# Softmax of a decode-attention step: eight accumulating exps replaced by one shift on VectorE, two whole-tile exps on ScalarE and a sum on VectorE

## The chip, the cores and the metric

The kernel runs on one core of one Trainium2 chip. The metric is the device time of one execution in microseconds (us), as a median of runs. A ratio is the mean time of one kernel's fast runs over that of the other's of the same rounds, so it is not quite the ratio of the medians that are quoted beside it.

Engine names in the profile: PE is the matrix engine, PEld its weight loads, DVE is VectorE, ACT is ScalarE, SPq is the queue that issues the loads. "L691" is a line of the kernel. PSUM is the memory that PE writes its results to here, SBUF the on-chip memory that the loads fill. The span is the length of the profiled execution. The granted clock is the share of its full clock that PE was given; "full clock" below means 1.00.

## The reference, cut to what matters

One token goes through a modulated layer norm, attention over a long cache, and a gated FFN. Attention is the large part: 32 query heads share 4 K/V heads of 65,536 rows.

```python
q = (h @ wq)                                   # 32 heads of 128, one row
scores = einsum('bhqd,bhkd->bhqk', q, k) * 128 ** -0.5     # k: 4 heads x 65536 x 128, each shared by 8 heads
p = softmax(scores, axis=-1)
o = einsum('bhqk,bhkd->bhqd', p, v)
x = x + ga * (o @ wo)
h = layernorm(x) * (1 + cb) + sb
out = x + gb * ((gelu(h @ w_gate) * (h @ w_up)) @ w_down)
```

Every byte of K, V and the weights is used once.

## The kernel before

The cache is worked off in 32 steps. A step takes 64 K tiles and 64 V tiles of 128x128 (2 MB of K and 2 MB of V) for 8 heads. PE transposes the K tiles in four groups T(0..3), DVE (three groups) and ACT (one) move them from PSUM to SBUF, and PE then computes the scores QK into one PSUM bank and, after the exps, P times V. Stages of three steps are interleaved:

```python
# PE, step i: T and MT/MB belong to i and i-1, QK to step i-1, PV to step i-2
T(0); QK(0); T(1); QK(1); PV(0); T(2); QK(2); QK(3); PV(1); T(3); PV(2); MT(); PV(3); MB()
# PV(0) waits for the V load and for ex, the exps of its step
```

```python
# DVE and ACT, step i (cut)
E(0)                                   # DVE: evict 16 transposed K tiles
OC()                                   # DVE: copy out an attention output
E(1); E(2)                             # DVE
# with j = i - 1; the scores lie in sc_ps[:, (j % 2) * 512 : +512] as (tile n, head h)
m1[s].done(dve.tensor_reduce(m_col[:, j % 2, :].unsqueeze(2), scv, AX.X, ALU.max))
...                                    # max over partitions through PE (MT, MB)
v_mc[j] = DVE.done(dve.tensor_copy(mneg[:, j, :], b6[:, 256:256 + REP]))   # -scale * max, on all partitions
E(3)                                   # ACT: evict the last 16 tiles
AC.wait(v_mc[j], pt.get(("PV", j - SITES)))
for h in range(REP):                   # REP = 8 heads
    ins = act.activation(
        p_sb[:, s, :, h], scv[:, h, :], ACT.Exp,
        bias=mneg[:, j, h:h + 1], scale=scale, accum_out=z_all[:, j, h:h + 1],
    )
ex[s].done(ins)
```

The loads go through one queue in a fixed order into ten 2 MB slots. A load is issued as soon as PE has released its slot:

```python
def issue_ready():
    while issued[0] < len(loads):
        j = loads[issued[0]]
        if any(q.freed is None for q in j.prev):
            return
        SP.wait(*(q.freed for q in j.prev))
        sp.dma_start(j.view, j.src).then_inc(j.tok[0], 16)
        issued[0] += 1
```

## Time and profile before

| | before |
|---|---|
| median | 440.44 us (440.28 to 440.68) |
| profiled span | 438.8 us |
| read from HBM | 185.60 MB |
| PE / DVE / ACT busy | 351.7 / 176.2 / 146.4 us |

These lines of the profile page give the busy time of each engine, the bytes, and by fortieths of the span (in tenths) the granted PE clock and the busy share of the DMA engines.

```profile
PE 351.7 (80%) x7107; PEld 318.4 (73%) x7107; DVE 176.2 (40%) x300; ACT 146.4 (33%) x553; POOL 11.7 (3%) x25
...
PEclk9955555959777986869955899556995597659855
DMA  8999999999999999999999999999999999999995
...
HBM read 185.60 MB, written 0.00 MB: 423 GB/s over the span
```

PE has the highest busy share of the compute engines, but the row of the DMA is the one that is full from the first slice to the last but one. The windows view has the exact numbers: window, then busy time of PE, PEld, DVE, ACT and POOL with instruction counts, then the granted clock, the DMA share and GB/s.

```profile
200.00:225.00 25.00, 20.55 (x478) 20.02 (x478) 12.42 (x20) 11.89 (x51) 0.00 (x0) 0.87 1.01 432
225.00:250.00 25.00, 25.00 (x485) 24.72 (x484) 11.48 (x17) 9.21 (x35) 0.00 (x0) 0.59 1.01 436
...
388.00:392.00 4.00, 1.33 (x28) 1.20 (x29) 3.15 (x6) 0.00 (x0) 0.00 (x0) 0.50 1.01 429
```

In the first window PE idles for 4.5 us; in the second, at a granted clock of 0.59, it is busy throughout; in the third PE has almost nothing to do, because the softmax is being closed. The DMA moves about 430 GB/s in all three. The Trainium skill, "DMA: Bandwidth & Descriptors", section Specifications, names 435 GB/s as the ceiling of the fabric; the trace's 429 to 436 GB/s lie at it (other windows of 15 and 25 us read up to 442, so page and trace agree to about 2%).

What the change removes is this pair of groups (line, engine, operation, output and input, count; then busy time and mean ns of one; then the idle time before them):

```profile
L691 ACT ACTIVATE p_sb<-sc_ps,mneg 128x64 bf16<-128x64 f32 x256 | 83.5, 560 | 3.9 <-DVE mneg L686 3.9
L691 ACT ACTIVATION_READ_ACCUMULATOR p_sb<-sc_ps,mneg 128x1 f32 x256 | 77.1, 365 | 0.0
```

The two groups overlap in time, so they are not to be added: the timeline shows one exp starting every 0.29 us. Here are the ends of one step's exps and what stands behind them (timeline: start, duration, instruction):

```profile
209.14 0.54 ACT L691 ACTIVATE p_sb<-sc_ps,mneg 128x64 bf16<-128x64 f32 x1
...
211.36 0.39 ACT L691 ACTIVATION_READ_ACCUMULATOR p_sb<-sc_ps,mneg 128x1 f32 x1
...
211.85 0.54 PE L625 MATMUL b<-p_sb,slots 128*128 128x8 bf16 x16 [0.58 <-issue]
```

PE sat idle for 0.58 us before its first PV matmul, until just after the eighth exp's accumulator was read (211.36 + 0.39 = 211.75 us). So the exps are taken to be on PE's path in this step (the profile names no releaser, `<-issue`; the times fit).

PE's waits, longest in total first (engine, line, what it waited for: us in total, times, longest):

```profile
PE b L625 <- DMA slots<-in_A_v_cache_dram: 11.2, 12, 2.0
...
PE kt_ps L561 <- DMA slots<-in_A_k_cache_dram: 10.3, 5, 5.1
...
PE b L625 <- issue: 6.4, 8, 2.4
...
PE b L625 <- ACT p_sb L691: 3.0, 1, 3.0
```

PE waits 21.5 us for K and V loads in the loop and at most 9.4 us for the exps.

### The profile page before, as it was taken

The numbers are of one execution on the slowest core, as the hardware profiler recorded it, in microseconds if no ns is written. First come the engines' busy times: TensorE is split into PE (matmuls) and PEld (weight loads), VectorE is DVE, ScalarE is ACT, GpSimd is POOL, SyncE is SP. The second block draws the span as 40 slices with busy tenths as digits, with TensorE's granted clock in tenths as the row PEclk, the third lists the DMA queues.
The fourth block names the chain that finished last, engine by engine and source line by source line (L and its number), as shares of the span: only waits on it lengthen the run. The fifth ranks groups of instructions, "written<-read, shape, count | busy, mean of one in ns | idle before, by whom it ended". The sixth has DMA issues, their size and how long they took to land.

```text
span 438.8 us, 15336 instructions
## 1 busy us (share of the span) xinstructions
PE 351.7 (80%) x7107; PEld 318.4 (73%) x7107; DVE 176.2 (40%) x300; ACT 146.4 (33%) x553; POOL 11.7 (3%) x25
## 2 busy tenths in 40 slices
PE   0547449998989889898799989999989999557554
PEld 0214139998989879798799989899988999434234
DVE  4102013545444644455444466345563365142100
ACT  1000001343435634344613553444654434600000
POOL 8100000000000000000000000000000000000000
PEclk9955555959777986869955899556995597659855
DMA  8999999999999999999999999999999999999995
GB/s 332 427 435 428 430 429 432 432 433 425 430 445 420 453 414 455 408 445 438 410 448 415 445 419 442 427 435 432 430 437 424 439 423 433 432 427 431 424 425 237
DMA packets 11957, 185.89 MB, mean 424 GB/s; under 512 B 1568, under 2 KB 1568, under 8 KB 1952
## 3 DMA queue, kind: packets, MB, share of 16 engines
q1 hardware_dynamic: 11632, 185.61, 98.8%
q8 instruction: 13, 0.21, 0.2%
q10 hardware_dynamic: 304, 0.01, 0.0%
q14 instruction: 8, 0.07, 0.0%
HBM read 185.60 MB, written 0.00 MB: 423 GB/s over the span
## 4 chain that ended last, share of the span: by engine, by line
DMA 60%; PE 35%; DVE 2%; issue 1%; SPq 1%; ACT 1%; POOL 0%
DMA slots<-in_A_v_cache_dram 39%; PE kt_ps L561 18%; DMA slots<-in_A_k_cache_dram 10%; DMA slots<-in_B_w_down_dram 7%; PE b L625 7%; PE sc_ps L581 6%; DMA slots<-in_w_mod_dram 4%; PE kt_ps L392 2%; PE b L605 1%; SPq L234 1%; PE b L372 1%; ACT p_sb L691 1%; PE b L595 1%; DVE kt_sb L751 0%; PE sc_ps L453 0%
## 5 line engine op out<-in xcount | busy, mean ns | idle before, releaser
L561 PE MATMUL kt_ps<-ident,slots 128*128 128x128 bf16 x2048 | 179.5, 258 | 11.0 <-DMA slots<-in_A_k_cache_dram 10.3
L561 PEld LDWEIGHTS kt_ps<-ident,slots 128*128 128x128 bf16 x2048 | 154.9, 118 | 12.7 <-issue 9.8
L660 DVE COPY kt_sb<-kt_ps 128x2048 bf16<-128x2048 bf16 x96 | 117.6, 1225 | 108.6 <-PE kt_ps L561 108.5
L660 ACT ACTIVATE kt_sb<-kt_ps 128x2048 bf16<-128x2048 bf16 x32 | 60.1, 1877 | 183.3 <-PE kt_ps L561 183.3
L625 PE MATMUL b<-p_sb,slots 128*128 128x8 bf16 x2176 | 75.8, 168 | 20.6 <-DMA slots<-in_A_v_cache_dram 11.2
L625 PEld LDWEIGHTS b<-p_sb,slots 128*128 128x128 bf16 x2176 | 69.8, 100 | 23.3 <-DMA slots<-in_A_v_cache_dram 12.3
L691 ACT ACTIVATE p_sb<-sc_ps,mneg 128x64 bf16<-128x64 f32 x256 | 83.5, 560 | 3.9 <-DVE mneg L686 3.9
L691 ACT ACTIVATION_READ_ACCUMULATOR p_sb<-sc_ps,mneg 128x1 f32 x256 | 77.1, 365 | 0.0
L581 PE MATMUL sc_ps<-q_buf,kt_sb 128*128 128x8 bf16 x2112 | 69.9, 167 | 0.5 <-issue 0.5
L581 PEld LDWEIGHTS sc_ps<-q_buf,kt_sb 128*128 128x128 bf16 x2112 | 67.9, 100 | 0.6 <-issue 0.6
L392 PE MATMUL kt_ps<-slots,h_pad 128*32 128x512 bf16 x176 | 17.1, 510 | 14.3 <-DMA slots<-in_A_wq_dram 6.3
L684 DVE TENSOR_REDUCE mg<-b 8x1 f32<-8x128 f32 x32 | 8.9, 279 | 37.1 <-PE b L595 37.1
L679 DVE TENSOR_REDUCE m_col<-sc_ps 128x8 f32<-128x512 f32 x32 | 21.8, 681 | 4.7 <-PE sc_ps L581 4.7
L392 PEld LDWEIGHTS kt_ps<-slots,h_pad 128*32 128x32 bf16 x176 | 5.0, 112 | 24.1 <-DMA slots<-in_A_wq_dram 8.3
L392 PE MATMUL kt_ps<-slots,s_pad 128*32 128x512 bf16 x96 | 12.5, 553 | 9.3 <-DMA slots<-in_w_mod_dram 9.3
L392 PEld LDWEIGHTS kt_ps<-slots,s_pad 128*32 128x32 bf16 x96 | 3.6, 119 | 17.3 <-DMA slots<-in_w_mod_dram 12.6
L605 PE MATMUL b<-negi,mg 8*128 8x8 f32 x66 | 15.8, 309 | 0.0
L605 PEld LDWEIGHTS b<-negi,mg 8*128 8x128 f32 x66 | 12.7, 239 | 2.2
L453 PEld LDWEIGHTS sc_ps<-identf,kt_sb 128*128 128x128 f32 (+1 forms) x48 | 7.6, 204 | 8.2 <-DVE kt_sb L774 4.3
L453 PE MATMUL sc_ps<-identf,kt_sb 128*128 128x128 f32 (+1 forms) x48 | 9.1, 352 | 4.5 <-DVE kt_sb L774 2.4
L686 DVE COPY mneg<-b 128x8 f32<-128x8 f32 x32 | 5.3, 167 | 18.1 <-PE b L605 18.1
L372 PE MATMUL b<-u_col,slots 128*128 128x1 bf16 x224 | 6.6, 165 | 6.5 <-DMA slots<-in_B_w_down_dram 5.9
(97 smaller groups left out, 84.9 us busy)
## 6 DMA issues: line engine op xcount, KB each, us to landing
slots<-in_A_k_cache_dram SPq DMA_DIRECT2D x16, 4096.0 KB, 20.3
slots<-in_A_v_cache_dram SPq DMA_DIRECT2D x32, 2048.0 KB, 26.5
slots<-in_w_mod_dram SPq DMA_DIRECT2D x8, 1536.0 KB, 17.5
slots<-in_A_wq_dram SPq DMA_DIRECT2D x4, 2048.0 KB, 35.2
slots<-in_A_wo_dram SPq DMA_DIRECT2D x4, 2048.0 KB, 32.5
slots<-in_B_w_gate_dram SPq DMA_DIRECT2D x4, 1792.0 KB, 21.9
slots<-in_B_w_up_dram SPq DMA_DIRECT2D x4, 1792.0 KB, 23.6
slots<-in_B_w_down_dram SPq DMA_DIRECT2D x3, 2048.0 KB, 29.1
```

What stands on the lines that cost most here:

```text
L372: ins = pe.matmul(bank[:, j:j + 1], view[:, kk, j * P:(j + 1) * P], rhs[:, k0 + kk:k0 + kk + 1], start=first, stop=True, skip_group_check= ...
L392: ins = pe.matmul(out, pad[:, k, :], jb.view[:, kk, c0:c0 + ROW], start=k <= last_k[0], stop=k >= last_k[1], skip_group_check=True,)
L453: ins = pe.transpose(dst[:, i * w:i * w + n], src[:, a], identf[0:src.shape[0], 0:n])
L561: ins = pe.transpose(kt_ps[:, half * 2048 + t * P:half * 2048 + (t + 1) * P], j_k[i - i % KU].view[:, i % KU * CH + b * TB + t, :], ident[ ...
L581: ins = pe.matmul(sc_ps[:, base + n * REP:base + (n + 1) * REP], kt_sb[:, j % 2, n, :], q_buf[:, j % SITES, :], start=True, stop=True,)
L605: ins = pe.matmul(b6[:, 256:256 + REP], mg8[:, j % 2:j % 2 + 1].to_broadcast([REP, P]), negi[:, :], start=True, stop=True,)
L625: ins = pe.matmul(b7[:, s * REP:(s + 1) * REP], j_v[j].view[:, n, :], p_sb[:, s, n, :], start=(n == 0), stop=(n == CH - 1),)
L660: ev[i % SITES][b].done(act.activation(dst, src, ACT.Copy) if E_ is AC else dve.tensor_copy(dst, src))
L679: m1[s].done(dve.tensor_reduce(m_col[:, j % 2, :].unsqueeze(2), scv, AX.X, ALU.max))
L684: m2[s].done(dve.tensor_reduce(mg8[:, j % 2:j % 2 + 1], b6[0:REP, 32:32 + P], AX.X, ALU.max))
L686: v_mc[j] = DVE.done(dve.tensor_copy(mneg[:, j, :], b6[:, 256:256 + REP]))
L691: ins = act.activation(p_sb[:, s, :, h], scv[:, h, :], ACT.Exp, bias=mneg[:, j, h:h + 1], scale=scale, accum_out=z_all[:, j, h:h + 1],)
```

## The change

Its intent is to relieve ACT. All 8 heads get their own maximum subtracted by DVE in one pass over the score tile in PSUM, in place. ACT then needs no bias and no accumulator, so one instruction covers all 8 heads: one exp writes P as bf16 and a second writes the exp as f32 back into PSUM, and DVE sums that one. Sixteen ACT records a step become two; DVE gets two passes over 128x512 f32.

```diff
+            def Z():
+                j = i - 2
+                if not 0 <= j < NC:
+                    return
+                zv = sc_ps[:, (j % 2) * 512:(j % 2) * 512 + CH * REP].rearrange("p (n h) -> p h n", h=REP)
+                DVE.wait(v_ze[j])
+                v_z[j] = DVE.done(dve.tensor_reduce(z_all[:, j, :].unsqueeze(2), zv, AX.X, ALU.add))
+
             E(0)
             OC()
             E(1)
+            Z()
             E(2)
...
                 v_mc[j] = DVE.done(dve.tensor_copy(mneg[:, j, :], b6[:, 256:256 + REP]))
+                DVE.wait(v_mc[j])
+                v_sh = DVE.done(dve.scalar_tensor_tensor(
+                    scn.rearrange("p (n h) -> p n h", h=REP), scn.rearrange("p (n h) -> p n h", h=REP), scale,
+                    mneg[:, j, :].unsqueeze(1).to_broadcast([P, CH, REP]), ALU.mult, ALU.add))
             E(3)
             if 0 <= j < NC:
-                AC.wait(v_mc[j], pt.get(("PV", j - SITES)))
-                for h in range(REP):
-                    ins = act.activation(
-                        p_sb[:, s, :, h], scv[:, h, :], ACT.Exp,
-                        bias=mneg[:, j, h:h + 1], scale=scale, accum_out=z_all[:, j, h:h + 1],
-                    )
-                ex[s].done(ins)
+                AC.wait(v_sh, pt.get(("PV", j - SITES)))
+                ex[s].done(act.activation(p_sb[:, s, :, :].rearrange("p n h -> p (n h)"), scn, ACT.Exp))
+                v_ze[j] = AC.done(act.activation(scn, scn, ACT.Exp))
```

(Cut: the definition of `scn`, the score tile of step j, two empty dictionaries, and the wait for the last sum before the final rescaling.)

More of the change, by code (lines that the diff above doesn't have):

```diff
@@ L648, in emit_all @@
         v_mc = {}
+        v_ze = {}
+        v_z = {}
         def others_step(i):
@@ L685, in others_step @@
                 DVE.wait(pt[("MB", j)])
+                scn = sc_ps[:, (j % 2) * 512:(j % 2) * 512 + CH * REP]
                 v_mc[j] = DVE.done(dve.tensor_copy(mneg[:, j, :], b6[:, 256:256 + REP]))
+                DVE.wait(v_mc[j])
+                v_sh = DVE.done(dve.scalar_tensor_tensor(
+                    scn.rearrange("p (n h) -> p n h", h=REP), scn.rearrange("p (n h) -> p n h", h=REP), scale,
+                    mneg[:, j, :].unsqueeze(1).to_broadcast([P, CH, REP]), ALU.mult, ALU.add))
             E(3)
             if 0 <= j < NC:
-                AC.wait(v_mc[j], pt.get(("PV", j - SITES)))
-                for h in range(REP):
-                    ins = act.activation(
-                        p_sb[:, s, :, h], scv[:, h, :], ACT.Exp,
-                        bias=mneg[:, j, h:h + 1], scale=scale, accum_out=z_all[:, j, h:h + 1],
-                    )
-                ex[s].done(ins)
+                AC.wait(v_sh, pt.get(("PV", j - SITES)))
+                ex[s].done(act.activation(p_sb[:, s, :, :].rearrange("p n h -> p (n h)"), scn, ACT.Exp))
+                v_ze[j] = AC.done(act.activation(scn, scn, ACT.Exp))
         PE.wait(t1, v_negi, v_q, v_zero)
@@ L732, in emit_all @@
         v_w = AC.done(act.activation(w_all[:, :, :], w_all[:, :, :], ACT.Exp))
-        DVE.wait(v_w, *(ex[i % SITES].tok(seen_by(i)) for i in range(NC - SITES, NC)))
+        DVE.wait(v_w, v_z[NC - 1])
         v = DVE.done(dve.tensor_tensor(z_all[:, :, :], z_all[:, :, :], w_all[:, :, :], ALU.mult))
```

## The prediction

> **What bounds the kernel now.** The DMA. The page counts 185.6 MB read; from 5 us to 432 us the windows view gives a DMA share of 0.98 to 1.04 in every stretch, through attention loop, softmax tail (384 to 404 us) and FFN. 185.6 MB at the loop's about 431 GB/s is 430.6 us; the slow first 5 us and the 5.3 us after the last weights land (433.5 us) make up the rest of the 438.8 us span. The Trainium skill, "DMA: Bandwidth & Descriptors", Specifications, gives a fabric ceiling of 435 GB/s; the trace sits at it. PE (80% busy) is a close second: a loop step (about 9.7 us of DMA for 4.19 MB) takes PE 8.0 to 8.6 us at full clock, 11.1 us at the granted 0.5; the queue's slack of about 10 us (K loads take 20.3 us to landing, 9.7 us of it their own) evens this out. DVE (40%) and ACT (33%) have room.
>
> **What the change does per step (32 steps).**
> - Removed on ACT: 8 exps of 128x64 with accumulator reads, 2.63 us together (chain of waits).
> - Added on ACT: two 128x512 exps. A 128x512 f32 ACT copy out of PSUM takes 0.597 us, so about 1.1 to 1.2 us together. ACT busy falls from 146 to about 102 us.
> - Added on DVE: the shift in PSUM, 0.69 us (as the 128x512 f32 PSUM copy), and the sum, 0.68 us (as the max over the same tile with the same stride). DVE busy rises from 176 to about 220 us (50%).
> - P is ready about 1.4 us after the max instead of 2.6.
>
> **How much is on the critical path.** Little. At full clock PE waits 0.6 us a step for the exps before the first PV (timeline, 211.2 to 211.8 us); at clock 0.5 not at all. So PE's full-clock steps shrink by 0.6 us, but PE then only waits longer for the next K or V load, since the DMA is full. In the tail the last exps shorten by about 1.2 us (381.2 to 383.9 us); the FFN is gated by weights landing until 433.5 us, so this too is swallowed.
>
> **New costs that could show.** At full clock the shift ends about 209.5 us, where the next step's first eviction on DVE starts at 209.6. The sum stands between second and third eviction: 1.23 + 0.68 = 1.9 us against the 1.75 us that PE needs there, so the third eviction and the max slip 0.15 us, against 0.45 us of slack. At half clock there are 3 us of room. I expect no DMA starvation.
>
> **Prediction: 440.2 us, 8 in 10 between 439.0 and 441.8.** Faster by over 2%: 0.01; within 2%: 0.97; slower: 0.02.
>
> **What would show it.** DMA share still 0.98 to 1.04 in every loop window and the last weights landing at 433 to 434 us; ACT busy about 100, DVE about 220 us; shift and sum near 0.69 us; PE's wait for the exps gone and its waits for K and V loads grown by as much; last-ending chain still mainly DMA.
>
> **What would make it wrong.** (1) Longer DMA waits leave PE idle longer and its granted clock (mean 0.733) falls; if it runs at 0.5 for several pairs of steps, slots are freed late and DMA windows drop below 0.97: slower. (2) Shift or sum cost about twice as much (strided view, PSUM read and write in one pass), pushing evictions and PE. [...]

## The result, and the profile after

| | before | after |
|---|---|---|
| median of 6 runs | 440.44 us | 440.53 us (440.32 to 440.67) |
| ratio of fast runs | | 1.0001 (95%: 0.9989 to 1.0014) |
| PE / DVE / ACT busy | 351.7 / 176.2 / 146.4 us | 347.2 / 216.3 / 100.4 us |

Nothing changed in the time. Executions over 1.5% slower than the fastest of the same kernel are left out of the means. The page's rows after, the same as shown before:

```profile
PE 347.2 (79%) x7107; PEld 310.8 (71%) x7107; DVE 216.3 (49%) x364; ACT 100.4 (23%) x105; POOL 11.7 (3%) x25
...
PEclk9955558886677886968579599887859989568655
DMA  8999999999999999999999999999999999999995
...
HBM read 185.60 MB, written 0.00 MB: 423 GB/s over the span
```

46 us of ACT work went, 40 us of DVE work came, and the DMA row is the same to the digit. The windows shown before have, after:

```profile
200.00:225.00 25.00, 23.74 (x436) 23.32 (x437) 14.48 (x24) 7.94 (x9) 0.00 (x0) 0.60 1.01 433
225.00:250.00 25.00, 22.89 (x547) 22.42 (x546) 16.12 (x25) 7.67 (x7) 0.00 (x0) 0.84 1.02 437
...
388.00:392.00 4.00, 3.94 (x40) 1.64 (x44) 0.00 (x1) 0.00 (x0) 0.00 (x0) 0.50 0.99 420
```

The new groups cost what same-sized passes had cost before:

```profile
L706 ACT ACTIVATE p_sb<-sc_ps 128x512 bf16<-128x512 f32 x32 | 19.1, 597 | 19.0 <-DVE sc_ps L700 19.0
L700 DVE SCALAR_TENSOR_TENSOR sc_ps<-sc_ps,mneg 128x512 f32<-128x512 f32 x32 | 22.4, 700 | 1.1
L678 DVE TENSOR_REDUCE z_all<-sc_ps 128x8 f32<-128x512 f32 x32 | 21.8, 681 | 2.2 <-ACT sc_ps L707 2.2
...
L707 ACT ACTIVATE sc_ps<-sc_ps 128x512 f32<-128x512 f32 x32 | 18.9, 592 | 0.0
```

PE's waits after:

```profile
PE kt_ps L561 <- DMA slots<-in_A_k_cache_dram: 15.4, 6, 5.1
PE b L625 <- DMA slots<-in_A_v_cache_dram: 13.9, 13, 2.1
...
PE b L625 <- ACT p_sb L706: 2.4, 2, 1.7
```

The waits for K and V loads rose from 21.5 to 29.3 us. One step of the changed kernel's timeline shows the exchange:

```profile
259.48 0.60 ACT L706 ACTIVATE p_sb<-sc_ps 128x512 bf16<-128x512 f32 x1 [0.32 <-DVE sc_ps L700]
...
260.88 0.54 PE L581 MATMUL sc_ps<-q_buf,kt_sb 128*128 128x8 bf16 x16
...
262.34 0.56 PE L625 MATMUL b<-p_sb,slots 128*128 128x8 bf16 x16 [0.92 <-DMA slots<-in_A_v_cache_dram]
```

P was complete at 260.08 us, before PE had even finished the QK group ahead of it, and the first PV matmul still had to wait 0.92 us, now for the V load. The attention as a whole did end earlier: the last step's maximum is spread over the partitions (L605) at 377.01 us in place of 380.40, and the first eviction after the output projection starts at 394.15 us in place of 397.97. That too was swallowed. Part of it went into the gate's matmuls, of which 56 in a row took 5.32 us in place of 3.63 at a lower granted clock; the rest went into PE's wait for the up-projection's weights, which grew from 6.1 to 7.5 us. From there on the two kernels are level (the second group of up-projection matmuls starts at 410.44 us before and 410.31 after), and the spans are 438.8 and 439.1 us.

### The profile page after: what moved, and what is told of

Same layout as the page of the kernel before. It is cut to its first block, busy times and chain, and to the rows that moved or that the text cites. A ratio compares the mean times of both kernels' runs of the same rounds, so it can differ in the third digit from the quotient of the medians.

```text
span 439.1 us, 14950 instructions
## 1 busy us (share of the span) xinstructions
PE 347.2 (79%) x7107; PEld 310.8 (71%) x7107; DVE 216.3 (49%) x364; ACT 100.4 (23%) x105; POOL 11.7 (3%) x25
## 3 DMA queue, kind: packets, MB, share of 16 engines
HBM read 185.60 MB, written 0.00 MB: 423 GB/s over the span
## 4 chain that ended last, share of the span: by engine, by line
DMA 60%; PE 34%; DVE 2%; issue 1%; SPq 1%; ACT 0%; POOL 0%
DMA slots<-in_A_v_cache_dram 39%; PE kt_ps L561 17%; DMA slots<-in_A_k_cache_dram 10%; DMA slots<-in_B_w_down_dram 7%; PE b L625 6%; PE sc_ps L581 6%; DMA slots<-in_w_mod_dram 4%; PE kt_ps L392 2%; PE b L605 1%; SPq L234 1%; PE b L372 1%; PE b L595 1%; DVE sc_ps L700 0%; DVE kt_sb L763 0%; ACT p_sb L706 0%
## 5 line engine op out<-in xcount | busy, mean ns | idle before, releaser
L561 PE MATMUL kt_ps<-ident,slots 128*128 128x128 bf16 x2048 | 173.0, 252 | 16.1 <-DMA slots<-in_A_k_cache_dram 15.4
L561 PEld LDWEIGHTS kt_ps<-ident,slots 128*128 128x128 bf16 x2048 | 149.3, 115 | 17.9 <-issue 9.1
L625 PEld LDWEIGHTS b<-p_sb,slots 128*128 128x128 bf16 x2176 | 68.4, 99 | 20.2 <-DMA slots<-in_A_v_cache_dram 15.0
L392 PE MATMUL kt_ps<-slots,h_pad 128*32 128x512 bf16 x176 | 19.6, 571 | 15.9 <-DMA slots<-in_B_w_up_dram 7.5
L706 ACT ACTIVATE p_sb<-sc_ps 128x512 bf16<-128x512 f32 x32 | 19.1, 597 | 19.0 <-DVE sc_ps L700 19.0
L700 DVE SCALAR_TENSOR_TENSOR sc_ps<-sc_ps,mneg 128x512 f32<-128x512 f32 x32 | 22.4, 700 | 1.1
L678 DVE TENSOR_REDUCE z_all<-sc_ps 128x8 f32<-128x512 f32 x32 | 21.8, 681 | 2.2 <-ACT sc_ps L707 2.2
L392 PE MATMUL kt_ps<-slots,s_pad 128*32 128x512 bf16 x96 | 13.6, 589 | 8.1 <-DMA slots<-in_w_mod_dram 8.1
L707 ACT ACTIVATE sc_ps<-sc_ps 128x512 f32<-128x512 f32 x32 | 18.9, 592 | 0.0
L605 PE MATMUL b<-negi,mg 8*128 8x8 f32 x66 | 14.9, 295 | 0.0
L786 DVE COPY kt_sb<-kt_ps 128x512 f32<-128x512 f32 x3 | 2.1, 692 | 23.9 <-PE kt_ps L392 23.9
```

The costliest lines, as they stand in the source:

```text
L392: ins = pe.matmul(out, pad[:, k, :], jb.view[:, kk, c0:c0 + ROW], start=k <= last_k[0], stop=k >= last_k[1], skip_group_check=True,)
L561: ins = pe.transpose(kt_ps[:, half * 2048 + t * P:half * 2048 + (t + 1) * P], j_k[i - i % KU].view[:, i % KU * CH + b * TB + t, :], ident[ ...
L605: ins = pe.matmul(b6[:, 256:256 + REP], mg8[:, j % 2:j % 2 + 1].to_broadcast([REP, P]), negi[:, :], start=True, stop=True,)
L625: ins = pe.matmul(b7[:, s * REP:(s + 1) * REP], j_v[j].view[:, n, :], p_sb[:, s, n, :], start=(n == 0), stop=(n == CH - 1),)
L678: v_z[j] = DVE.done(dve.tensor_reduce(z_all[:, j, :].unsqueeze(2), zv, AX.X, ALU.add))
L700: v_sh = DVE.done(dve.scalar_tensor_tensor(scn.rearrange("p (n h) -> p n h", h=REP), scn.rearrange("p (n h) -> p n h", h=REP), scale, mneg ...
```

## Experiments

Theory A: the DMA alone sets the time. The change makes PE's step shorter, and the loads take the gain back. Theory B: compute matters as much, and the change's gain on ACT is cancelled by as large a loss on DVE. Theory C: PE bounds part of the loop, in the stretches with a low granted clock. All but `after_split`, `after_z3` and the two kernels with more exps give a wrong attention. They too passed the comparison with the reference's output, so a pass says little about the attention (presumably because its contribution to the output is small, which was not measured); this holds for the changed kernel as well, whose sum was checked by reading, and not by a test that would see it.

### Half of the K and V bytes: lite_before, lite_after, lite_after_noz

The loads after the first four steps bring half of their bytes, and the compute stays as it is: of V the first 32 of a step's 64 tiles, of K, whose load covers two steps, all tiles of the first step and none of the second. PE works on what the slots held before in place of the rest. 126.88 MB are read in place of 185.60. In both kernels:

```diff
-            sp.dma_start(j.view, j.src).then_inc(j.tok[0], 16)
+            sp.dma_start(j.dst, j.src).then_inc(j.tok[0], 16)   # dst, src: first half for K and V of steps >= 4
```

and in `lite_after_noz` also

```diff
-                v_z[j] = DVE.done(dve.tensor_reduce(z_all[:, j, :].unsqueeze(2), zv, AX.X, ALU.add))
+                v_z[j] = DVE.done(dve.tensor_copy(z_all[:, j, :], zv[:, :, 0]))
```

> The kernel before with the K and V loads after the first four steps cut to half (about 61 MB fewer; result wrong on purpose, compute unchanged). If the DMA alone sets the time of the kernel before (theory A), the loop now runs at PE's own pace of 8.0 to 8.6 us a step where the granted clock is full, instead of 9.7 us: 385 to 415 us, DMA share in the loop 0.5 to 0.7, PE waiting about 0.6 us a step for the exps. If DMA and compute bound it equally (theory B), at most 10 us are saved: 430 or more.

> The changed kernel with the same cut loads. Theory A: here the 0.6 us a step that the change takes out of PE's wait for the exps is no longer given back to the loads, so it is 12 to 22 us (3 to 5%) faster than the kernel before with cut loads, and PE's wait for the exps is near zero. Theory B (a gain on ACT cancelled by as large a loss on DVE): within 1% of the kernel before with cut loads.

> As the changed kernel with cut loads, and the DVE sum replaced by a copy of 8 elements (wrong result on purpose), so DVE has 0.5 us less a step. Theory A with the slack that the prediction gives it (0.15 us slip against 0.45 us): within 1% of the changed kernel with cut loads. Theory B: 10 us or more faster than it, since the sum is then what takes the gain back.

| | median | ratio to the kernel before |
|---|---|---|
| lite_before | 397.92 us | 0.9023 (0.9004 to 0.9043) |
| lite_after | 371.06 us | 0.8405 (0.8377 to 0.8432) |
| lite_after_noz | 371.59 us | 0.8439 (0.8422 to 0.8457) |

With fewer bytes the kernel before gets 42.7 us faster (440.62 us in the same rounds), so the loads had held it back. And now the change is worth 26.9 us (0.8405 / 0.9023 = 0.9315, 6.9% faster), which is more than the 12 to 22 us that were expected. Theory B falls: gain and loss do not cancel. The sum on DVE costs nothing that could be measured (lite_after_noz is not faster). The windows view shows the limit having moved to PE; first `lite_before`, then `lite_after` (columns as above):

```profile
155.00:185.00 30.00, 28.45 (x684) 27.93 (x685) 17.02 (x25) 13.54 (x55) 0.00 (x0) 0.89 0.59 244
```

```profile
155.00:185.00 30.00, 29.82 (x798) 29.31 (x796) 24.11 (x38) 12.14 (x13) 0.00 (x0) 1.00 0.71 286
```

PE idles 1.55 us of 30 before and 0.18 us after, and the DMA is only 59% and 71% busy. The step can be timed between two consecutive transposes of the maximum (PE L599) at full clock. `lite_before`:

```profile
203.32 0.27 PE L599 MATMUL b<-identf,m_col 128*8 128x128 f32 x1
...
207.60 0.54 PE L629 MATMUL b<-p_sb,slots 128*128 128x8 bf16 x16 [0.34 <-issue]
...
211.40 0.27 PE L599 MATMUL b<-identf,m_col 128*8 128x128 f32 x1
```

and `lite_after`:

```profile
201.31 0.27 PE L599 MATMUL b<-identf,m_col 128*8 128x128 f32 x1
...
204.46 0.54 PE L585 MATMUL sc_ps<-q_buf,kt_sb 128*128 128x8 bf16 x16
...
204.87 0.54 PE L629 MATMUL b<-p_sb,slots 128*128 128x8 bf16 x16
205.27 1.05 PE L565 MATMUL kt_ps<-ident,slots 128*128 128x128 bf16 x16
205.80 0.68 DVE L682 TENSOR_REDUCE z_all<-sc_ps 128x8 f32<-128x512 f32 x1
...
206.40 1.21 DVE L666 COPY kt_sb<-kt_ps 128x2048 bf16<-128x2048 bf16 x1
...
208.66 0.27 PE L599 MATMUL b<-identf,m_col 128*8 128x128 f32 x1
```

A full-clock step takes 8.08 us in the first and 7.35 us in the second: 0.73 us less. (With all bytes it takes 8.08 us in the kernel before, too, from 207.57 to 215.65 us, so the cut loads did not change PE's pace.) PV now follows QK after 0.41 us with no wait. The third eviction (206.40) starts 0.08 us after its transposes end (205.27 + 1.05 = 206.32), against 0.04 us in `lite_before`, so the sum in front of it has delayed it by some 0.04 us. But not every step runs at full clock. The same 27 steps of the loop with cut loads take 230.9 us in the profile of `lite_before` (108.95 to 339.86 us) and 204.1 us in that of `lite_after` (110.93 to 315.03 us), 26.8 us less. Of these, 27 x 0.73 = 19.7 us are the shorter step. The other 7.1 us go with the granted clock: steps below full clock added 12.8 us in `lite_before` and 5.7 us in `lite_after`, and the mean clock rose from 0.823 to 0.856. That the change caused this is not shown. The expected 12 to 22 us had counted a gain of 0.6 us in each full-clock step and nothing from the clock.

### Less PE work at full bytes: after_half_pv

```diff
-                    for t in range(TB):
+                    for t in range(0, TB, 2):          # PV only (and stop at the last n used)
```

> The changed kernel with all its loads, but only every second matmul of P times V (wrong result on purpose): PE loses about 35 us of busy time, 1.0 us a step. Theory A: within 0.5% of the kernel before, 439 to 442 us, PE's waits for loads 20 to 35 us longer. If PE still bounds part of the loop (theory C: throttled stretches where PE is slower than the loads), it is 2 to 6 us faster or more.

Measured: 440.39 us, ratio 0.9997 (0.998 to 1.0014). PE's busy time fell from 347.2 to 315.8 us, and its waits for loads rose to 52.4 us:

```profile
PE kt_ps L561 <- DMA slots<-in_A_k_cache_dram: 42.5, 13, 6.9
...
PE b L625 <- DMA slots<-in_A_v_cache_dram: 9.9, 14, 1.9
```

Thirty-one microseconds of PE work taken away are worth nothing. Theory C falls, too, for the changed kernel, on which this was run: no stretch of the loop is bound by PE in a way that the queue does not even out.

### More work, to find where the room ends: after_z3, lite_after_z3, before_exp12, before_exp16

Two further sums into a spare tile in each step of the changed kernel (both with all loads and with half):

```diff
+                for k in range(2):
+                    dve.tensor_reduce(zjunk[:, k, :].unsqueeze(2), zv, AX.X, ALU.add)
```

and 4 or 8 further exps with accumulators ahead of the 8 of the kernel before:

```diff
+                for h in range(4):                      # 8 in before_exp16
+                    act.activation(pjunk[:, h, :], scv[:, h, :], ACT.Exp,
+                        bias=mneg[:, j, h:h + 1], scale=scale, accum_out=rz[:, h:h + 1])
```

> The changed kernel with the DVE sum done three times (two into a spare tile): DVE has 1.36 us more a step, 44 us in all, and stays correct. Theory A: the third eviction slips by about 1.4 us in full-clock steps, PE's step grows to about 9.0 to 9.5 us, still under the 9.7 us of the loads: 440 to 443 us. Theory B: slower by 20 us or more.

> The changed kernel with cut loads and the DVE sum done three times. With all loads this cost 0.16 per cent. With compute as the limit the third eviction slips by about 1.3 us and the max with it, against 0.45 us of slack, so a full-clock step grows from 7.35 to about 8.1 to 8.3 us: 393 to 405 us, PE waiting about 0.8 us a step for the max. If DVE had no part in PE's pace, it would stay at 371 us.

> The kernel before with 12 exps with accumulators a step in place of 8 (four go to a spare tile first): P is ready about 1.17 us later, result correct. Theory A: full-clock PE steps grow from about 8.6 to 9.8 us, just the pace of the loads, throttled ones (11.1 us, 1.3 us of slack) hardly: 440 to 446 us. Theory B: slower by 20 us or more.

> The kernel before with 16 exps a step in place of 8: P is ready about 2.34 us later. Now the full-clock step is about 10.9 us, over the 9.7 us of the loads, so both theories expect it clearly slower; theory A 470 to 490 us with the DMA share of the loop down to about 0.85 to 0.9; theory B about 440 + 32 x 2.3 = 514 us.

| | extra per step | median | ratio to the kernel before |
|---|---|---|---|
| after_z3 | 1.36 us DVE | 441.18 us | 1.0016 (1.0 to 1.0033) |
| lite_after_z3 | 1.36 us DVE | 412.61 us | 0.9351 (0.9325 to 0.9377) |
| before_exp12 | 1.17 us until P | 446.41 us | 1.012 (1.01 to 1.0141) |
| before_exp16 | 2.34 us until P | 493.34 us | 1.1203 (1.1184 to 1.1222) |

The same two sums cost 0.7 us with all bytes (the interval of the ratio starts at 1.0) and 41.5 us with the cut loads. That is theory A in one pair: what is swallowed under the loads shows where the loads are not the limit. The room is not endless, though. Four exps more cost 6.0 us and eight more 52.9 us. Three of these four runs lie above the expected ranges of theory A: 446.41 us (440 to 446), 493.34 us (470 to 490) and `lite_after_z3` with 412.61 us (393 to 405). With eight exps more PE is so late in freeing slots that the DMA itself goes short, in this window of `before_exp16`:

```profile
250.00:275.00 25.00, 22.81 (x415) 22.33 (x412) 10.32 (x18) 15.02 (x80) 0.00 (x0) 0.57 0.85 357
```

The granted clock is part of this: its mean was 0.733 in the profile of the kernel before, 0.705 with 12 exps and 0.618 with 16. PE waits for the exps 18 times in all with 12 exps (31.0 us) and in every step with 16 (43.7 us): 12.7 us more wait, but 46.9 us more time. PE's busy time, for the same matmuls, rose from 359.7 to 396.8 us with the lower clock. The expectations had not reckoned with a lower clock. That the waits lower the clock is not shown: after_half_pv waits for loads even longer, and its mean clock was 0.727 to 0.765. The same pattern is seen in `lite_after_z3`: its full-clock step is 8.17 us, as expected (two transposes of the maximum at 202.82 and 210.99 us), 0.82 us more than that of `lite_after`. The same 27 steps as above take 245.2 us in place of 204.1; 22.1 of these 41.1 us are the longer full-clock step, and the other 19.0 go along with a mean clock of 0.778 in place of 0.856.

### Which part of the removed work mattered: lite_before_noacc

```diff
-                        bias=mneg[:, j, h:h + 1], scale=scale, accum_out=z_all[:, j, h:h + 1],
+                        bias=mneg[:, j, h:h + 1], scale=scale,
```

> The kernel before with cut loads, its 8 exps kept but without accumulators (row sums set to 1, wrong on purpose): one part of the change alone. In the cut-loads pair the full-clock step fell from 8.08 to 7.35 us. If the accumulator reads are the larger part of what the 8 exps cost PE (theory D), nearly all of that 0.7 us goes here too: 370 to 378 us. If it is the number of instructions (theory E), the pitch of 0.29 us falls only to about 0.24 us, 8 exps take about 2.2 us in place of 2.6, and it lands midway: 382 to 390 us.

Measured: 391.51 us, ratio 0.8874 (0.886 to 0.8887). Both expectations miss: without the accumulators only some 6.6 of the 26.9 us are gained (by the ratios, 0.9023 less 0.8874). Even less comes from the step itself: at full clock it takes 8.00 us (transposes of the maximum at 202.27 and 210.27 us) in place of 8.08; the rest goes with the mean clock, 0.839 in place of 0.823. The timeline shows why:

```profile
211.84 2.55 ACT L696 ACTIVATE p_sb<-sc_ps,mneg 128x64 bf16<-128x64 f32 x8
```

Eight exps alone still take 2.55 us, a pitch (from one start to the next) of 0.29 us as with accumulators ((2.55 - 0.54) / 7). In the step of `before` shown above, the last accumulator read ends at 211.75 us and the last exp at 211.74 (211.16 + 0.58), so leaving the reads out takes nothing off the end. The accumulator reads lay under the exps; what cost PE its time is the pitch of the eight exps. The whole-tile exp differs from them in the count of instructions, in the bias operand, and in reading and writing without a stride (each small exp takes every eighth element). The stride of the output is not the reason: the added exps of `before_exp16` write to adjacent addresses, take 0.34 us where those that write p_sb take 0.58, and still start 0.29 us apart, as the others do:

```profile
261.11 0.34 ACT L694 ACTIVATE w_all<-sc_ps,mneg 128x64 bf16<-128x64 f32 x1
...
261.40 0.34 ACT L694 ACTIVATE w_all<-sc_ps,mneg 128x64 bf16<-128x64 f32 x1
...
261.68 0.58 ACT L699 ACTIVATE p_sb<-sc_ps,mneg 128x64 bf16<-128x64 f32 x1
...
261.97 0.59 ACT L699 ACTIVATE p_sb<-sc_ps,mneg 128x64 bf16<-128x64 f32 x1
```

Count, bias operand and the stride of the input were not taken apart. The Trainium skill, "ScalarE: Activation LUTs", section "What ACT_TABLE_LOAD costs", gives 280 ns + 0.833 ns per element for an ACTIVATE with a pointer bias and an overlap of about 93 ns back to back, which makes about 240 ns for these 64 elements (an estimate from that page). The measured pitch of 287 ns is longer. For a single small exp the page's figures give 280 + 0.833 x 64 = 333 ns: those into adjacent addresses took 323 ns on average in `before_exp16`, those into p_sb 560 ns in `before`, with the same pitch, so the overlap is no fixed 93 ns here. For the whole-tile exp without a pointer operand its 186 ns + 0.833 x 512 = 612 ns (an estimate from that page) agrees with the 597 ns of the trace to 3%.

### A version that would beat both: after_split

Since the loads set the time, only bytes and the two ends of the kernel are left to gain from. The last 2 MB load of the down-projection's weights was cut into two of 1 MB:

```diff
+            w = 2 if b + 3 < NBF else 1
+            for q in range(0, 2, w):                   # the last pair of blocks as two loads
```

> The changed kernel with the last 2 MB load of the down weights cut into two of 1 MB. In the profile of the changed kernel the last 96 matmuls all start when that load lands (433.81 us), though half of its bytes should be there some 2.4 us before. Then 32 of the 96 are done early and the end comes about 0.9 us sooner: 439.3 to 440.0 us, ratio about 0.998. If the loads land out of order or the tail has another limit: unchanged.

Measured: 440.45 us, ratio 1.0 (0.9987 to 1.0014). The timeline's end shows what I had misread:

```profile
433.73 1.01 PE L374 MATMUL b<-u_col,slots 128*128 128x1 bf16 x32 [1.49 <-DMA slots<-in_B_w_down_dram]
...
434.96 0.97 PE L374 MATMUL b<-u_col,slots 128*128 128x1 bf16 x24 [0.23 <-DMA slots<-in_B_w_down_dram]
...
436.20 0.38 PE L374 MATMUL b<-u_col,slots 128*128 128x1 bf16 x8 [0.26 <-DMA slots<-in_B_w_down_dram]
```

The split did what it should (32 matmuls ran at 431.22 us), but the last loads, of 512, 256 and 256 KB, land later, the last one at about 436.2 us, and only 8 matmuls are left behind it. In the unsplit kernels the matmuls of the large load hid these waits; that the bytes arrive as late there can be seen in the windows view of `before`, which still has 51 GB/s after 434 us (by single microseconds, 88 GB/s from 435 to 436 us and none from 436 to 437):

```profile
434.00:438.80 4.80, 2.77 (x85) 2.31 (x82) 0.61 (x3) 0.00 (x0) 0.00 (x0) 0.50 0.14 51
```

The kernel is bound by its loads to within about 2.8 us of its end (span 439.0 us). No version that beats both was found.

## Why the prediction was right

- "What bounds the kernel now. The DMA." Right, and shown by three runs: cut loads gave 42.7 us, 31 us less PE work gave nothing, 44 us more DVE work gave 0.7 us.
- Costs of the parts: the shift was predicted at 0.69 us and took 0.700, the sum 0.68 and 0.681, the two exps 1.1 to 1.2 together and 1.09 in the timeline (the second starts 0.50 us after the first). ACT busy 102 and 100.4 us, DVE 220 and 216.3 us. Reading the cost of a new pass from an old pass of the same shape and memory was good to about 2%.
- "PE's full-clock steps shrink by 0.6 us" was too small: the step shrank by 0.73 us (8.08 to 7.35 us). The idle time that the profile writes beside an instruction (0.58 us) starts at the modelled end of the matmuls before, which overlap (PE counts as busy for 7.49 us of the 8.08 us step, but for all of the 7.35 us one); the distance of starts is the better measure.
- "P is ready about 1.4 us after the max instead of 2.6": counted alike, from the end of the copy of the maximum, it was 1.37 us (258.71 to 260.08 us) in place of 2.95 (208.80 to 211.75). The 2.6 us are the exps alone; before them lay 0.34 us in which ACT was still evicting the last K tiles (207.37 + 1.88 = 209.25 us).
- "The third eviction and the max slip 0.15 us": it slipped by some 0.04 us. The slack was enough either way.
- "PE's wait for the exps gone and its waits for K and V loads grown by as much": in the two profiles the waits for the exps fell from 9.4 to at most 4.0 us (2.4 of them in the last two steps, where no other work is left to cover them), and those for loads grew by 7.8 us (21.5 to 29.3). The sizes do not match, because PE's busy time also fell, by 4.5 us at a mean clock of 0.753 in place of 0.733, and the attention ended some 3.4 us earlier. The exchange itself is as predicted, but with all bytes there was little to exchange: 0.58 us in each of 7 steps, and 2.9 us in the last two. How many steps would have this wait was not in the prediction.
- "The 5.3 us after the last weights land (433.5 us)" was a misreading: the last wait that could be seen ended there, bytes still arrived until about 436 us (seen in after_split and in the windows of the kernel before). It did not touch the outcome.
- Of the ways to be wrong, (1) was not met: the mean clock was 0.733 to 0.754 in six runs of the changed kernel, against 0.725 to 0.771 in the fast runs of the kernel before beside the experiments. Longer waits for loads did not lower it in after_half_pv either (0.727 to 0.765), so this worry was unfounded for waits of that kind; what sets the clock stays open. (2) did not happen: shift and sum took 0.700 and 0.681 us.

## What to carry to other kernels

Look at the DMA's share in every window before costing a change to the compute: where it was full throughout here, a change that frees 0.7 us of a full-clock step was worth nothing, and one that adds 1.4 us to an engine with room cost next to nothing, as long as PE still freed its slots in time (2.3 us more before P did not fit, and cost 52.9 us). To learn what such a change is worth by itself, cut the loads and run the pair again; here the 0.0% became 6.9%, so the change may still pay once fewer bytes are read. Eight small exps cost mostly by the 0.29 us from one start to the next and not by their elements (64 each; a single one of 512 took 0.60 us): one pass over all heads after a broadcast subtraction took P from 2.95 us after the maximum to 1.37.

## What the Trainium skill lacked or had wrong

- "TensorE: Matmul & The Clock Gate", Part 1, says that the clock drops after at least one idle window of about 3.4 us. In lite_before the clock fell at about 158 us (16 transposes took 1.87 us in place of 1.05, and the window from 160 to 165 us has 0.52) although PE's idle times in the timeline from 125 us on had been at most 0.58 us, once a step of 8 us. Such drops came every 34 us, four steps, up to 329 us. In lite_after, with gaps of at most 0.2 us, windows of 60 us from 125 to 305 us had 0.94 to 1.00, but the clock still dropped three times (at 193, 225 and 292 us). The page's rule does not cover this. Its section "A second HAM failure mode: psum-queue depth-cycling" tells of a kernel whose frequent short idle times make the clock oscillate, which is nearer, but gives no length or share of idle time. The cause stays open.
- "ScalarE: Activation LUTs" gives no cost for reading the accumulator behind an ACTIVATE. Here it was hidden behind the next exp (pitch 0.29 us with and without it), and the pitch of small exps with a pointer bias was 287 ns against about 240 ns from the page's figures. Nor has it a figure for an output with a stride: an exp took 560 ns into every eighth bf16 element in `before` and 323 ns into adjacent ones in `before_exp16`, with the same pitch.
- "DMA: Bandwidth & Descriptors", section "Where 436 GB/s comes from", says that the HBM side (about 358 GB/s) binds for transfers between HBM and SBUF. For this kernel on one core that is wrong: the trace has 429 to 436 GB/s from HBM in the windows shown, and 423 GB/s over the whole span; the fabric's figure is the one that fits. The page's own table of measured loads has 425 GB/s for one core alone and keeps about 358 for two that share the memory; the sentence lacks this condition.
